# A fixed task order, w3 and w4 in groups of two token blocks, and block transposes by DMA through DRAM instead of TensorE

## The chip, the cores and the metric

The kernel runs on one core of one Trainium2 chip. The metric is device time in microseconds (us), the median of several executions. In this text PE is TensorE (PEld its weight loads), DVE is VectorE, ACT is ScalarE, POOL is GpSimd and SP is SyncE, whose queue issues the DMAs. "SPq" in the profile is SP's sequencer while it issues.

## The reference

```python
def _A_ref(q, k, v, shift_k, ssm_k, ssm_D):       # S = 2048 tokens, D = 512
    ...                                           # k_shift: causal taps of k, 4 wide
    kv = k_shift * v
    y = irfft(rfft(pad(kv)) * rfft(pad(ssm_k)))[:S]        # long convolution, per channel
    y = y + kv * ssm_D
    return q * y

def _B_ref(x, w1, w2, w3, w4):                    # F = 1792
    h = gelu(layernorm(x) @ w1)
    hs = concat(four quarters of h, moved by +1, -1, +2, -2 tokens) @ w2
    x1 = x + hs
    return x1 + gelu(layernorm(x1) @ w3) @ w4

x = A_q
h = x + _A_ref(layernorm(x), A_k, A_v, A_shift_k, A_ssm_k, A_ssm_D)
return h + _B_ref(layernorm(h), B_w1, B_w2, B_w3, B_w4)
```

## The kernel before

Tokens are held as 16 blocks of 128. The first half of the kernel (the "FFT stage") computes the convolution as matmuls with tables of sines. The second half has a mixer (inverse matmuls, gate, h, layernorm, w1, w2) and an MLP (layernorm, w3, w4). w1 and w3 contract over channels, so each of the 16 blocks of normed h ("hb") and of normed x1 ("lb") must be transposed first: 32 block transposes, each of four 128x128 pieces on PE into PSUM (`ptx`), then one copy to the buffer `rc` by ACT or DVE.

Each half is a list of tasks. A task names the engines that may run it with a cost in us, and a scheduler in the program picks the order while the kernel is built. The hardware then runs each engine's list in that order; an engine that waits for one task does not go around it.

```python
    plan = Plan({"mm": 6, "pt": 2, "lb": 6, "z": 4}, 300)     # second half; 300 rounds of list scheduling
    ...
    def transposes(key):
        def f(e):
            pt = tl[("pt",) + key] = ps_x.tile([P, DC, P], BF16, name="ptx", tag="ptx")
            for c in range(DC):
                nc.tensor.transpose(pt[:, c, :], tl[key][:, c * P:(c + 1) * P], ident[:])
        return f
    def tcopy(key, dstT, slot):
        def f(e):
            copy(e, dstT[:, :, slot * P:(slot + 1) * P], tl[("pt",) + key][:])
        return f
    def w3mm(g, fc):
        def f(e):
            pg = mm(("g", g, fc))
            for k in range(DC):                               # 512 tokens a matmul: four blocks
                nc.tensor.matmul(pg[:], lhsT=w3_sb[:, k, fc * P:(fc + 1) * P], rhs=lnT[:, k, g * 512:(g + 1) * 512],
                                 start=(k == 0), stop=(k == DC - 1))
        return f
    ...                                                       # cut
            for c in (b - 1, b):
                task(("hb", c), {"V": 0.33, "G": 1.0, "A": 0.71}, hbf(c), [("rr", p)])
                task(("LT", c), {"PE": 0.24}, transposes(("hb", c)), [("hb", c)], take="pt")
                task(("TE", c), {"A": 0.48, "V": 0.33}, tcopy(("hb", c), hnT, c), drop=("LT", c))
            for h in range(2):
                task(("W", p, h), {"PE": 0.92}, w1mm(p, h), [("TE", b - 1), ("TE", b)], take="mm")
    ...                                                       # cut; the same for lb with L, E and w3
```

## Time and profile before

| | before |
|---|---|
| median time | 244.74 us (4 runs, 244.01 to 246.14) |
| span of the profiled run | 241.9 us |
| PE busy | 225.2 us, 93% of the span |
| granted PE clock, mean | 0.979 |

First the profile page of the kernel before: busy time by engine, then the span in 40 slices with the busy tenths of PE and DVE and the granted PE clock.

```profile
PE 225.2 (93%) x1685; PEld 111.8 (46%) x1685; DVE 159.1 (66%) x328; ACT 138.1 (57%) x193; POOL 54.3 (22%) x98
...
PE   7999898869989985899999999999999999999994
...
DVE  6859998958999979999999952993522640012121
...
PEclk9999999979999999599999999999999999999999
```

The windows of the kernel before, one row per stage: start and end, then length, busy time and number of instructions of each engine, granted clock, DMA share, GB/s. The stages are the FFT stage, the turn to the mixer, the mixer up to the first w3, and the rest.

```profile
core 0: us, PE busy (x) PEld busy (x) DVE busy (x) ACT busy (x) POOL busy (x), PEclk, DMA share, GB/s
8.00:84.30 76.30, 69.02 (x722) 33.64 (x715) 66.29 (x96) 62.47 (x68) 14.88 (x18) 0.98 0.65 252
84.30:103.50 19.20, 15.15 (x130) 5.58 (x128) 16.97 (x43) 10.80 (x16) 9.39 (x15) 0.82 0.74 258
103.50:131.70 28.20, 28.11 (x265) 20.11 (x262) 27.01 (x71) 21.46 (x39) 17.34 (x31) 1.00 0.00 1
131.70:238.60 106.90, 106.65 (x537) 50.13 (x534) 43.40 (x91) 39.80 (x67) 10.16 (x17) 1.00 0.06 19
```

From 103.5 to 238.6 us PE is idle for only 0.3 us, while the DMA share is near zero (0.00 and 0.06). Work taken off PE there should shorten the kernel by its own length, and the DMA engines look like a free place to put it. The PE waits of the kernel before (who waited for whom: us in total, times, longest), of which these are the two longest:

```profile
PE pw L465 <- DMA rc<-ra: 2.5, 1, 2.5
PE mm L806 <- DVE rd L640: 2.5, 1, 2.5
```

And its block transposes by form (count, then busy us, mean ns of one, idle before; the lengths of matmuls in the trace overlap, so that four of 219 ns or more take only 0.22 us in the chain of waits):

```profile
L692 PE MATMUL ptx<-ident,rd 128*128 128x128 bf16 x64 | 6.1, 230 | 0.6 <-ACT rd L678 0.6
L692 PE MATMUL ptx<-ident,lb 128*128 128x128 bf16 x64 | 5.5, 219 | 0.1
```

Those four, 0.22 us of PE, are one block's worth.

### The profile page before, as it was taken

What the parts mean: (1) busy time and instruction counts of PE and PEld (TensorE: products, weight loads), DVE (VectorE), ACT (ScalarE), POOL (GpSimd) and SP (SyncE); (2) the same over time, 40 slices, a digit from 0 to 9 for tenths busy, and PEclk for the clock granted to TensorE, in tenths of its full rate; (3) what the DMA queues carried; (4) which work ended last, traced back from release to release, by engine and by line L of the source; (5) the groups of instructions that cost most, each with busy time, mean ns of one, the idle gap of its engine ahead of it and who ended that gap; (6) DMA issues with size and microseconds to landing.
All of it is one profiled execution on the core that took longest, in us unless ns stands there. A gap on an engine that the chain in (4) does not pass through costs nothing.

```text
span 241.9 us, 4308 instructions
## 1 busy us (share of the span) xinstructions
PE 225.2 (93%) x1685; PEld 111.8 (46%) x1685; DVE 159.1 (66%) x328; ACT 138.1 (57%) x193; POOL 54.3 (22%) x98
## 2 busy tenths in 40 slices
PE   7999898869989985899999999999999999999994
PEld 2576443433333432367676455445444444444441
DVE  6859998958999979999999952993522640012121
ACT  3953778869999974589657854254300266611000
POOL 3741303000100222996651420161000000000000
PEclk9999999979999999599999999999999999999999
DMA  6999827961363569600000000001011100000111
GB/s 165 396 420 427 335 83 310 388 267 43 133 217 130 168 213 391 191 0 3 0 3 0 1 0 3 0 1 43 3 43 43 43 3 0 0 22 24 43 43 43
DMA packets 11046, 28.07 MB, mean 116 GB/s; under 512 B 1809, under 2 KB 5650, under 8 KB 9490
## 3 DMA queue, kind: packets, MB, share of 16 engines
q1 hardware_dynamic: 10208, 26.74, 29.1%
q0 software_dynamic: 288, 1.05, 1.7%
q8 instruction: 13, 0.21, 0.3%
q10 hardware_dynamic: 530, 0.01, 0.1%
q14 instruction: 7, 0.06, 0.1%
HBM read 13.11 MB, written 2.10 MB: 63 GB/s over the span
## 4 chain that ended last, share of the span: by engine, by line
PE 65%; DVE 16%; DMA 10%; ACT 4%; issue 2%; POOL 2%; ACTq 0%; SPq 0%; DVEq 0%; POOLq 0%
PE mm L786 19%; PE mm L771 17%; DMA rb<-in_A_v_dram 5%; PE mm L706 5%; PE pv L554 5%; PE mm L731 4%; PE ptx L692 3%; PE pw L465 3%; DVE xk L441 3%; DMA ssk_bf<-in_A_shift_k_dram 3%; DVE st L635 3%; PE mm L618 3%; DVE q_sb L736 2%; DMA rc<-ra 2%; DVE qst L511 1%
## 5 line engine op out<-in xcount | busy, mean ns | idle before, releaser
L777 ACT ACTIVATE ra<-mm 128x512 bf16<-128x512 f32 x56 | 33.3, 596 | 47.9 <-PE mm L771 47.8
L771 PE MATMUL mm<-rc,rb 128*128 128x512 bf16 x224 | 51.1, 379 | 0.0
L786 PE MATMUL mm<-rt,ra 128*128 128x512 bf16 x224 | 49.3, 379 | 0.0
L794 DVE TENSOR_TENSOR ob<-mm,rd 128x512 bf16<-128x512 f32 x16 | 11.1, 692 | 54.1 <-PE mm L786 54.0
L786 PEld LDWEIGHTS <-ra 128*128 128x128 bf16 x224 | 21.9, 98 | 26.2
L771 PEld LDWEIGHTS <-rb 128*128 128x128 bf16 x224 | 21.5, 98 | 24.1
L326 ACT CAST rb<-pw 128x1024 bf16<-128x1024 f32 x16 | 16.3, 1064 | 2.6 <-PE pw L465 2.6
L554 PE MATMUL pv<-rb,rt 64*128 64x512 bf16 x128 | 16.5, 378 | 0.4 <-ACT rb L326 0.3
L706 PE MATMUL mm<-rc,rf 128*128 128x256 bf16 x128 | 16.1, 273 | 0.1
L731 PE MATMUL mm<-rf,rb 128*128 128x512 bf16 x64 | 15.8, 379 | 0.0
L736 DVE SCALAR_TENSOR_TENSOR q_sb<-rd,cr,mm 128x512 bf16<-128x512 bf16 x16 | 11.6, 727 | 5.6 <-PE mm L731 5.6
L432 PE MATMUL pk<-diag,rb 128*128 128x256 bf16 (+3 forms) x112 | 15.0, 288 | 0.2
L465 PEld LDWEIGHTS <-rf 128*64 128x64 bf16 x128 | 7.3, 116 | 14.9 <-issue 11.3
L326 ACT CAST ra<-pc 128x1024 bf16<-128x1024 f32 x13 | 12.5, 1023 | 2.3 <-PE pc L387 1.3
L706 PEld LDWEIGHTS <-rf 128*128 128x128 bf16 x128 | 12.2, 98 | 2.9 <-issue 0.6
L465 PE MATMUL pw<-rc,rf 128*64 128x512 bf16 x64 | 10.1, 407 | 3.6 <-DMA rc<-ra 2.5
L544 DVE TENSOR_TENSOR rb<-rb,rd 128x1024 bf16<-128x1024 bf16 x16 | 11.0, 685 | 3.6 <-ACT rb L326 3.6
L326 ACT COPY rc<-ptx 128x512 bf16<-128x512 bf16 x19 | 11.0, 592 | 3.9 <-PE ptx L692 3.9
L712 ACT ACTIVATE rb<-mm 128x512 bf16<-128x512 f32 x16 | 9.7, 618 | 6.0 <-PE mm L731 4.0
L629 ACT ACTIVATE z<-mm,qrs 128x512 f32<-128x512 f32 x16 | 10.3, 694 | 4.8 <-PE mm L618 4.4
L326 ACT CAST rc<-ph 128x1024 bf16<-128x1024 f32 x11 | 10.7, 1023 | 4.0 <-PE ph L387 3.9
L640 DVE SCALAR_TENSOR_TENSOR rd<-q_sb,qmv,z 128x512 bf16<-128x512 bf16 x16 | 11.8, 736 | 1.4 <-ACT z L629 1.4
(166 smaller groups left out, 342.3 us busy)
## 6 DMA issues: line engine op xcount, KB each, us to landing
rd<-rc SPq DMA_DIRECT2D x16, 256.0 KB, 4.5
rc<-ra SPq DMA_DIRECT2D x16, 256.0 KB, 3.3
ra<-rb SPq DMA_DIRECT2D x16, 256.0 KB, 2.5
ra<-in_A_ssm_k_dram SPq DMA_DIRECT2D x4, 512.0 KB, 6.8
ra<-in_A_k_dram SPq DMA_DIRECT2D x4, 512.0 KB, 8.8
rb<-in_A_v_dram SPq DMA_DIRECT2D x2, 1024.0 KB, 12.4
q_sb<-in_A_q_dram SPq DMA_DIRECT2D x2, 1024.0 KB, 10.6
out_dram<-ob SPq DMA_DIRECT2D x16, 128.0 KB, 1.8
```

Source lines behind the costliest of these rows:

```text
L326: nc.scalar.copy(o, i)
L432: nc.tensor.matmul(pk[:, i, P * (m + lo):P * (m + hi + 1)], lhsT=kT[:, c, b, 2:P + 2] if b >= 0 else kT[:, c, NB + b, 1:P + 1], rhs=diag[: ...
L465: nc.tensor.matmul(ps[64 * t:64 * t + 64, r, :], lhsT=ftab[:, kh, r, t, :], rhs=z[:, kh, t, :], start=True, stop=True)
L554: nc.tensor.matmul(ps[:, t, :], lhsT=tt[hs, min(x, 2), kh, :], rhs=pr[hs, x // 2, x % 2, :], start=(x == 0), stop=(x == 3))
L640: nc.vector.scalar_tensor_tensor(out=h_sb[:, b, :], in0=q_sb[:, b, :], scalar=qmv[:, b, 0:1], in1=tl["z", b][:], op0=SUB, op1=MUL)
L706: nc.tensor.matmul(pw_[:, j * 256:(j + 1) * 256], lhsT=w1_sb[:, k, m * P:(m + 1) * P], rhs=hnT[:, k, p * 256:(p + 1) * 256], start=(k == 0 ...
L731: nc.tensor.matmul(px[:], lhsT=shifted(m, b), rhs=w2_sb[:, m, :], start=(m == 0), stop=(m == DC - 1))
L736: nc.vector.scalar_tensor_tensor(out=x1[:, b, :], in0=hbm[:, b, :], scalar=tl["cr", b // 2][:, b % 2:b % 2 + 1], in1=tl["x", b][:], op0=MU ...
L771: nc.tensor.matmul(pg[:], lhsT=w3_sb[:, k, fc * P:(fc + 1) * P], rhs=lnT[:, k, g * 512:(g + 1) * 512], start=(k == 0), stop=(k == DC - 1))
L777: nc.scalar.activation(gbuf[:, g % 2, fc, :], tl["g", g, fc][:], ACT.Gelu_apprx_tanh)
L786: nc.tensor.matmul(po[:], lhsT=gbuf[:, g % 2, fc, i * P:(i + 1) * P], rhs=w4_sb[:, fc, :], start=(fc == 0), stop=(fc == FC - 1))
L794: nc.vector.tensor_tensor(out=ob[:], in0=tl["o", 4 * g + i][:], in1=xh1[:, b, :], op=ADD)
```

## The change

The intent is to take 20 of the 32 block transposes off the saturated PE: a block goes to a DRAM scratch by a plain store, and comes back by DMA with the transposition done on the way. The schedulers of both halves are replaced by one order over the whole kernel, made beforehand (by a search, it seems). Smaller w3 groups (two token blocks) let MLP work start earlier.

```diff
-    def solve(self):                      # and forward(), backward(): list scheduling
-        ...
     def emit(self):
-        best = self.solve()
-        for _, n in sorted(best[1]):
-            self.t[n]["fn"](best[3][n])
+        for x in ORDER.split():           # ORDER = "1D 3D 4D 12G 30P 7D ...": task number and engine
+            ...
+    HP, LP = 4, 2                         # first 4 mixer pairs and 2 MLP pairs stay on PE
+    scr = ctx.enter_context(tc.tile_pool(name="scr", bufs=1, space=DRAM)).tile([2 * NB, P, D], BF16, name="scr")
+    def stored(key, slot):
+        return lambda e: nc.sync.dma_start(scr[slot], tl[key])
+    def flipped(dstT, scr_lo, n, lo):
+        def f(e):
+            for c in range(DC):           # four transposing loads for a pair of blocks
+                nc.sync.dma_start_transpose(dstT[:, c, lo:lo + n * P],
+                                            scr[scr_lo:scr_lo + n, :, c * P:(c + 1) * P].rearrange("b p x -> (b p) x"))
+        return f
@@ mixer, and alike with L and E in the MLP @@
+                if p < HP:
+                    (LT on PE and TE by copy, as before)
+                else:
+                    task(("LT", c), {"D": 0.5}, stored(("hb", c), NB + c), [("hb", c)], lat=LAND)
+            if p >= HP:
+                task(("TE", b), {"D": 1.6}, flipped(hnT, NB + b - 1, 2, (b - 1) * P), [("LT", b - 1), ("LT", b)], lat=LAND)
@@ w3 @@
-    def w3mm(g, fc):                      # 4 groups of four blocks, 512 columns a matmul
+    def w3mm(g, f):                       # 8 groups of two blocks, 256 columns a matmul, two fc a PSUM bank
```

Cut: all the order but its start, costs retouched in other tasks, the q statistics and table load moved in the order, one dummy warm-up fewer, the first inverse matmuls split in two tasks.

## The prediction

> **What bounds the kernel before.** The windows by stage show TensorE as the limit nearly everywhere: from 103.5 to 238.6 us PE is busy 134.8 of 135.1 us, and the chain of waits gives it 65% of the span. From 8 to 84 us (FFT stage) it is busy 69 of 76 us; the waits list names gaps: 2.5 us for the exchange copies rc<-ra before the first pw, about 1 us each for xk, pc evictions and rd copies. The one large hole is 84.3 to 103.5 us: about 6 us of real inverse matmuls plus dummy warm-ups (L572, L806), waiting for the chain: last exchange landed about 88.5, gate z on ACT 89.2, h on DVE from 89.9, pow on POOL 95.1, hb on ACT 97.4, transpose 98.3. DVE is 95% busy from 90 to 140 us; each h block costs it 1.6 us in series.
>
> **What changes, costed.**
> 1. 20 of 32 blocks lose their PE transposes. Four take 0.22 us of PE in the chain of waits, so 20 x 0.225 = 4.5 us leave a saturated PE. Their PSUM copies (ACT 586 ns, DVE 425 ns) go too. The Trainium skill (VectorE: DVE Perf Modes, "The three transpose paths") gives 390 ns per 128x128 transpose on TensorE, 1309 ns by DMA; here PE pays only about 56 ns of issue each, so the exchange wins less than that table suggests.
> 2. Added: 20 stores to DRAM, 40 transposing loads. The trace has 1.8 us from issue to landing for a 128 KB store; the skill (DMA: Bandwidth & Descriptors, "Anatomy of one DMA") calls about 2 us fixed. I estimate 6 us from hb to transposed data, against about 1 us now. The DMA engines are idle there (share 0.00 at 103.5 to 131.7): bandwidth is free, latency is not.
> 3. w3 at 256 columns instead of 512: the 256-column w1 matmuls take 0.87 us per eight, the 512-column ones 0.864 per four. Cost about 0.5 us.
> 4. One order across both halves: more pg matmuls before the first pw, two fewer q statistics in the DVE-bound part, one dummy group fewer. I estimate 1 to 3 us out of the FFT gaps. Splitting the inverse gains almost nothing: its matmuls already waited singly.
>
> **Critical path.** The first h starts at the same place, less the FFT gain. The order finishes four h before the first statistics (before: three), 1.5 us later; W of the fifth pair waits for DMA, about 5 us later than before. So PE gets new holes of 2 to 4 us between 105 and 122 us, but w3 starts about 122 us instead of 131.7 and fills the rest. From there about 113 us of PE work remain, without reason to stall; the tail (w4, 0.7 us add, store) is unchanged. Sum: -4.5 (transposes) +0.5 (w3) -2 (FFT) +0.5 (holes against earlier w3) = -5.5 us.
>
> **Prediction: 239.5 us**, 8 times in 10 within 235 to 244.5. Faster by over 2%: 0.55; within 2%: 0.41; slower: 0.04.
>
> **What would show it.** PE transposes ptx fall from 128 to 48; pv ends 1 to 3 us earlier; PE windows show holes before the first w3 near 122 us, none after; store-to-transposed latency near 6 us; eight 256-column w3 matmuls at 0.87 us.
>
> **What would make it wrong.** Slower transposing DMAs: the order is fixed, so each late block stalls everything behind it on PE, and stores on the same queue wait too. Or the search found more of the FFT and 84 to 103 us gaps than I credit (then nearer 235). Or 256-column matmuls not hiding their weight loads (98 ns against 108).

## The result

The changed kernel takes 262.0 us (4 runs, 260.74 to 263.36), against 244.74 us before. Ratios here are the mean time of one kernel's fast runs over that of the other's in the same rounds, so they are not quite the ratio of the medians quoted: here 1.070, 95% interval 1.061 to 1.079. The change is 7% slower; a gain of 2% was predicted.

The profile page of the changed kernel, the same rows as before:

```profile
PE 228.2 (87%) x1807; PEld 129.9 (50%) x1825; DVE 154.4 (59%) x317; ACT 134.1 (51%) x186; POOL 50.4 (19%) x98
...
PE   7899999899999849876997876999999866999994
...
PEclk9999999999999999995699979899999999799999
```

Where PE stood at 9 without a break in the second half, there are now three dents, and the granted clock falls there too. The windows of the changed kernel: the FFT stage, the turn and first mixer blocks up to the first store, the mixer to the next stores, then two stretches to the end.

```profile
8.00:80.30 72.30, 69.15 (x723) 32.16 (x719) 65.17 (x94) 62.29 (x66) 14.08 (x18) 1.00 0.68 262
80.30:107.60 27.30, 21.13 (x223) 11.07 (x225) 26.12 (x72) 19.23 (x33) 15.38 (x27) 1.00 0.57 191
107.60:131.20 23.60, 18.59 (x109) 11.75 (x109) 15.64 (x36) 10.71 (x19) 7.66 (x16) 0.78 0.20 56
131.20:205.50 74.30, 67.29 (x434) 43.82 (x439) 33.32 (x74) 23.40 (x41) 10.97 (x20) 0.95 0.19 52
205.50:258.00 52.50, 46.57 (x290) 29.23 (x292) 8.44 (x14) 14.36 (x25) 0.00 (x0) 0.97 0.14 41
```

The FFT stage is better than before: pv ends at 80.3 us instead of 84.3, and the first h starts at 86.0 us instead of 89.9. All of the loss comes after the first store to DRAM at 107.6 us, in stretches where PE is idle and the DMA engines are four fifths idle as well. The PE waits of the changed kernel show who is waited for:

```profile
PE mm L665 <- DMA rc<-scr: 8.3, 10, 1.1
PE mm L732 <- DMA rc<-scr: 7.6, 8, 1.1
```

The transposes by form of the changed kernel show that 80 of the 128 did leave PE:

```profile
L641 PE MATMUL ptx<-ident,rd 128*128 128x128 bf16 x32 | 3.0, 220 | 3.8 <-ACT rd L627 2.9 <-POOL rd L629 0.9
L641 PE MATMUL ptx<-ident,lb 128*128 128x128 bf16 x16 | 1.8, 266 | 0.0
```

So the intended work is gone from PE; in its place no single wait for the scratch is longer than 1.1 us, but there are eighteen of them. The timeline of the changed kernel, PE and the DMA queue alone, around one pair (start, length, engine, line; in brackets the idle time before and what ended it), shows why:

```profile
start us, us, engine line op out<-in xcount [idle before <-releaser]
...
147.38 3.81 SPq L655 DMA_TRANSPOSE rc<-scr  x3
149.01 0.27 PE L665 MATMUL mm<-rc,rf 128*128 128x256 bf16 x1
149.80 0.27 PE L665 MATMUL mm<-rc,rf 128*128 128x256 bf16 x1 [0.52 <-DMA rc<-scr]
...
151.13 0.27 PE L665 MATMUL mm<-rc,rf 128*128 128x256 bf16 x1 [1.06 <-DMA rc<-scr]
151.29 0.52 SPq L756 DMA_DIRECT2D out_dram<-ob  x1
151.91 0.87 SPq L650 DMA_DIRECT2D scr<-lb  x2
152.34 1.01 PE L665 MATMUL mm<-rc,rf 128*128 128x256 bf16 x4 [0.93 <-DMA rc<-scr]
```

PE does one w1 matmul, waits, does the next: it marches at the beat of the queue, one of four column chunks every 1.2 to 1.3 us. The instructions on the scratch give the beat (duration of the issue in ns, min/median/max, first and last start), and the landing time from issue:

```profile
L655 SPq DMA_TRANSPOSE rc<-scr x40: 1104/1234/1961, 110.7 to 220.0; - x40
L650 SPq DMA_DIRECT2D scr<-lb x12: 332/400/523, 138.8 to 213.7; - x12
L650 SPq DMA_DIRECT2D scr<-rd x8: 332/396/879, 107.6 to 139.7; - x8
...
DMA to landing us min/median/max: 1.7/2.4/3.9
```

A transposing load holds the queue for 1.23 us, a plain store for 0.40. A pair of blocks so takes 4 x 1.23 = 4.9 us of queue where the task's cost says 1.6, and the 40 loads take 49 us in all, during which nothing else can be issued on that queue.

### The profile page after: what moved, and what is told of

The parts are those of the page before. It is cut to its first block, busy times and chain, and to the rows that moved or that the text cites. A ratio compares the mean times of both kernels' runs of the same rounds, so it can differ in the third digit from the quotient of the medians.

```text
span 261.4 us, 4638 instructions
## 1 busy us (share of the span) xinstructions
PE 228.2 (87%) x1807; PEld 129.9 (50%) x1825; DVE 154.4 (59%) x317; ACT 134.1 (51%) x186; POOL 50.4 (19%) x98
## 5 line engine op out<-in xcount | busy, mean ns | idle before, releaser
L732 PE MATMUL mm<-rc,rb 128*128 128x256 bf16 x448 | 56.0, 284 | 7.8 <-DMA rc<-scr 7.6
L738 ACT ACTIVATE ra<-mm 128x512 bf16<-128x512 f32 x56 | 32.5, 596 | 50.6 <-PE mm L732 50.6
L732 PEld LDWEIGHTS <-rb 128*128 128x128 bf16 x448 | 45.5, 102 | 18.4 <-issue 9.9
L665 PE MATMUL mm<-rc,rf 128*128 128x256 bf16 x128 | 20.1, 300 | 9.0 <-DMA rc<-scr 8.3
L665 PEld LDWEIGHTS <-rf 128*128 128x128 bf16 x128 | 13.3, 106 | 14.4 <-issue 11.7
L490 PE MATMUL pv<-rb,rt 64*128 64x512 bf16 x128 | 17.1, 377 | 1.4 <-ACT rb L265 0.9
L690 PE MATMUL mm<-rf,rb 128*128 128x512 bf16 x60 | 16.7, 405 | 1.2 <-ACT rb L671 0.7
L578 ACT ACTIVATE z<-mm,qrs 128x512 f32<-128x512 f32 x16 | 10.5, 689 | 5.6 <-PE mm L567 3.8
L609 POOL TENSOR_TENSOR rr<-uw,mhalf 128x4 f32<-128x4 f32 x8 | 9.6, 1197 | 18.1 <-DVE hm L598 18.1
L371 PEld LDWEIGHTS <-rb 128*128 128x128 bf16 x112 | 9.3, 98 | 7.5 <-issue 2.1
L265 ACT CAST rb<-pv 128x1024 bf16<-128x1024 f32 x12 | 12.8, 1099 | 0.0
L380 DVE TENSOR_TENSOR xk<-pk,rb 128x1024 bf16<-128x1024 f32 x8 | 9.8, 1223 | 3.4 <-DMA rb<-in_A_v_dram 1.6
## 6 DMA issues: line engine op xcount, KB each, us to landing
q_sb<-in_A_q_dram SPq DMA_DIRECT2D x2, 1024.0 KB, 10.5
```

The costliest lines, as they stand in the source:

```text
L265: nc.scalar.copy(o, i)
L371: nc.tensor.matmul(pk[:, i, P * (m + lo):P * (m + hi + 1)], lhsT=kT[:, c, b, 2:P + 2] if b >= 0 else kT[:, c, NB + b, 1:P + 1], rhs=diag[: ...
L490: nc.tensor.matmul(ps[:, t, :], lhsT=tt[hs, min(x, 2), kh, :], rhs=pr[hs, x // 2, x % 2, :], start=(x == 0), stop=(x == 3))
L578: nc.scalar.activation(z[:], tl["y", b][:], ACT.Identity, bias=1.0, scale=qrs[:, b:b + 1])
L665: nc.tensor.matmul(pw_[:, j * 256:(j + 1) * 256], lhsT=w1_sb[:, k, m * P:(m + 1) * P], rhs=hnT[:, k, p * 256:(p + 1) * 256], start=(k == 0 ...
L690: nc.tensor.matmul(px[:], lhsT=shifted(m, b), rhs=w2_sb[:, m, :], start=(m == 0), stop=(m == DC - 1))
```

## The experiments

The theory (A): the queue time of the transposing loads, which is a cost per instruction, makes every pair late, and the fixed order has nothing else for PE at those places. Rivals: (B) the fixed order or the 256-column w3 is itself bad; (C) the round trip through DRAM (store, landing, load, landing) is too slow, whatever the queue does.

| run | what | median us | ratio to before (95%) |
|---|---|---|---|
| after | the changed kernel | 262.0 | 1.070 (1.061 to 1.079) |
| r1_pe_same_order | all transposes on PE | 241.73 | 0.986 (0.981 to 0.991) |
| r2_plain_copy | plain loads, wrong data | 236.59 | 0.965 (0.962 to 0.968) |
| r3_merged | one transposing load a pair | 236.72 | 0.966 (0.959 to 0.974) |
| r4_split | eight a pair, single look | 307.53 | |
| r5_before_one_load | kernel before, one a pair | 242.43 | 0.989 (0.986 to 0.992) |
| r6_before_four_loads | kernel before, four a pair | 244.82 | 0.999 (0.995 to 1.004) |
| r7_from_sbuf | two a pair, no DRAM trip | 236.13 | 0.963 (0.960 to 0.967) |
| r11_more_dma | r7 with 24 blocks by DMA | 238.91 | 0.974 (0.969 to 0.979) |

**r1_pe_same_order.** The changed kernel with `HP, LP = 8, 8`; in the order, each store is replaced by its PE transposes and each load by copies (mixer on ACT, MLP on DVE).

> The changed kernel with all 32 block transposes back on TensorE; the fixed order and the two-block w3 groups stay. Theory A (the queue time of the transposing loads, 1.24 us each and 4.96 us a pair, makes PE wait): the FFT gain of about 3.9 us is kept, so 238 to 242 us. Rival B (the fixed order or the 256-column w3 is itself bad): 250 us or more.

Measured 241.73 us. Rival B falls: without the DMA path the order and the small groups are 1.4% faster than before. Its w3 matmuls start at 120.7 us, those of the kernel before at 131.5. (The order was not made anew for transposes on PE, so 241.73 us need not be the best that such a kernel can do.)

**r2_plain_copy.** Wrong data: the same stores, the same number of loads of the same bytes, but without transposition.

```diff
-                nc.sync.dma_start_transpose(dstT[:, c, lo:lo + n * P],
-                                            scr[scr_lo:scr_lo + n, :, c * P:(c + 1) * P].rearrange("b p x -> (b p) x"))
+                nc.sync.dma_start(dstT[:, c, lo:lo + n * P].rearrange("p (b x) -> p b x", b=n),
+                                  scr[scr_lo:scr_lo + n, :, c * P:(c + 1) * P].rearrange("b p x -> p b x"))
```

> Wrong result on purpose: each transposing load is a plain copy of the same bytes from the same DRAM scratch, same count, same waits. Theory A: the issue falls to 0.4 to 0.5 us each, a pair takes 2 us instead of 5, time 236 to 242 us. Rival C (the round trip through DRAM itself, store and landing of 2 us each, is too late for this order): 252 us or more. Rival B: near 262 us.

Measured 236.59 us, so 25 us come back when only the kind of load changes. Its line on the scratch (as above, with the landing time, which here and above is that of stores and loads together):

```profile
L655 SPq DMA_DIRECT2D rc<-scr x40: 360/465/548, 112.0 to 193.4; - x40
...
DMA to landing us min/median/max: 1.7/2.0/3.5
```

The loads hold the queue 0.47 us instead of 1.23, while the landing time is nearly the same: for the loads alone, the DMA lists of the two runs have medians of 2.2 us and 2.4. Rival C falls: the trip through DRAM stayed, and it costs this order nothing. The comparison with the reference passed this kernel although its data are wrong.

**r3_merged.** One transposing load for a pair, right data:

```diff
-            for c in range(DC):
-                nc.sync.dma_start_transpose(dstT[:, c, lo:lo + n * P],
-                                            scr[scr_lo:scr_lo + n, :, c * P:(c + 1) * P].rearrange("b p x -> (b p) x"))
+            nc.sync.dma_start_transpose(dstT[:, :, lo:lo + n * P], scr[scr_lo:scr_lo + n].rearrange("b p x -> (b p) x"))
```

> Right result: one transposing load per pair (256 rows by 512 columns) instead of four of 256 by 128. If the 1.24 us is a cost of the instruction: a pair takes 1.3 to 2 us of the queue, time 238 to 244 us, better than before. If it is a cost per transposed piece or byte: one issue lasts about 5 us, time stays 258 to 264 us.

**r4_split.** Eight a pair:

```diff
-                nc.sync.dma_start_transpose(dstT[:, c, lo:lo + n * P], ...)
+                for i in range(n):
+                    nc.sync.dma_start_transpose(dstT[:, c, lo + i * P:lo + (i + 1) * P], scr[scr_lo + i, :, c * P:(c + 1) * P])
```

> Right result: eight transposing loads per pair (128 rows by 128 columns each) instead of four. Cost per instruction: about 1.24 us each, 9.9 us a pair, time 285 us or more. Cost per piece or byte: about 0.65 us each, time 260 to 268 us.

Measured 236.72 us merged and 307.53 us split. The lines of the transposing loads, first of the merged kernel, then of the split one:

```profile
L654 SPq DMA_TRANSPOSE rc<-scr x10: 1227/1233/1330, 111.8 to 192.0; - x10
```

```profile
L656 SPq DMA_TRANSPOSE rc<-scr x80: 1093/1230/2531, 110.6 to 264.9; - x80
```

The issue lasts 1.23 us for 32 KB (128x128, split), 64 KB (256x128, changed kernel) and 256 KB (256x512, merged). The issue is thus a cost of the instruction, not of bytes or pieces. The landing does depend on the size: 2.4 us after issue for 64 KB and 3.3 for 256 KB. But a merged pair is there 3.3 us after its load begins, where the last of four loads, begun 3.7 us after the first, lands some 6.1 us after it. The same bytes moved with 10, 40 and 80 such instructions give 236.7, 262 and 307.5 us (the last a single look). The merged kernel did better than the 238 to 244 us expected of it. The windows of the merged kernel show that the dents are gone: PE is idle for less than 1 us between 108.4 and 131.2 us, and for 0.3 us in the 69 us after that.

```profile
8.00:80.30 72.30, 69.31 (x722) 32.22 (x719) 65.30 (x96) 62.33 (x66) 14.11 (x18) 1.00 0.67 263
80.30:108.40 28.10, 22.68 (x213) 11.78 (x215) 26.15 (x72) 18.48 (x32) 16.08 (x29) 0.88 0.54 184
108.40:131.20 22.80, 21.87 (x177) 16.30 (x178) 21.11 (x52) 16.48 (x29) 10.62 (x21) 1.00 0.30 77
131.20:200.00 68.80, 68.54 (x487) 47.92 (x490) 30.71 (x63) 26.71 (x46) 7.82 (x14) 1.00 0.26 68
```

**r5_before_one_load and r6_before_four_loads.** Here the DMA path alone is put into the kernel before, with its own scheduler and its four-block groups, for the same 20 blocks. The scheduler is told the measured queue cost: 1.3 us a pair for one load, 5.0 us for four.

```diff
+                else:
+                    task(("LT", c), {"D": 0.5}, stored(("hb", c), NB + c), [("hb", c)], lat=1.9)
+            if p >= HP:
+                task(("TE", b), {"D": 1.3}, flipped(...), [("LT", b - 1), ("LT", b)], lat=2.1)    # r6: 5.0 and lat=1.2
```

> The kernel before, its own scheduler and four-block w3 groups; only the same 20 blocks go through DRAM, with one transposing load per pair, and the scheduler is told the measured costs (1.3 us of queue a pair, 2.1 us to land). If the transposes themselves gain what they take from PE (4.5 us), 239 to 242 us. If the exchange is worth it only in the searched order, 244 us or more.

> As the run before, but with four transposing loads per pair as in the changed kernel, and the scheduler is told the true 5.0 us a pair. If an honest cost in the scheduler would have saved the change, 240 to 244 us. If 50 us of queue time in stretches with a deadline cannot be hidden, 246 to 256 us: slower than before, but less than the changed kernel's 262, whose order believed 1.6 us a pair.

Measured 242.43 and 244.82 us. Exchanging PE transposes for merged loads gains 1.1% by itself in this schedule, a little less than the 239 to 242 us expected. Four loads a pair gain nothing (0.999, interval 0.995 to 1.004), but they also lose nothing when the scheduler knows what they cost: 40 issues of 1.24 us are in that trace too, and its PE waits list has none for the scratch. The time fell between my two expectations, close to the 240 to 244 us for an honest cost, and below the 246 to 256 us for a cost that cannot be hidden. So the cost of the instruction alone does not explain the 17 us that the changed kernel lost against the kernel before: the order matters too. That it was the 1.6 us in place of 4.9 which made the order so sensitive is argued, not shown: r6 differs from the changed kernel also in its scheduler and its w3 groups, and neither was the fixed order made anew with the true cost, nor the scheduler told the wrong one.

**r7_from_sbuf.** From the merged kernel, the store and the scratch go; each block is transposed straight from on-chip memory, two loads a pair.

```diff
-        return lambda e: nc.sync.dma_start(scr[slot], tl[key])
+        return lambda e: None
-            nc.sync.dma_start_transpose(dstT[:, :, lo:lo + n * P], scr[scr_lo:scr_lo + n].rearrange("b p x -> (b p) x"))
+            for i, key in enumerate(keys):
+                nc.sync.dma_start_transpose(dstT[:, :, lo + i * P:lo + (i + 1) * P], tl[key])
```

> The merged kernel without the trip through DRAM: each block is transposed by one load straight from on-chip memory (two transposing loads a pair, no stores). Queue time a pair 2.5 us against 2.0 with the stores, latency about 2 us less. If the DRAM trip is off the critical path, as the merged kernel's lack of PE waits for DMA says, 235 to 238.5 us. If the trip still costs (rival C), 234 us or less. If a block with an on-chip source costs more than 1.24 us, slower than 239.

Measured 236.13 us, the same as the merged kernel within noise. The trip through DRAM is off the critical path, as r2 said, and is not needed. With this source the instruction costs the same:

```profile
L655 SPq DMA_TRANSPOSE rc<-lb x12: 1190/1216/1716, 129.4 to 188.8; - x12
L655 SPq DMA_TRANSPOSE rc<-rd x8: 1200/1257/1924, 108.0 to 133.3; - x8
```

**r8_verify, r9_verify_control, r10_verify_sbuf.** As r2 passed with wrong data, passing proves little about a transposition. These three have a test at the end. Each of the 20 blocks is read back from the scratch, transposed on PE and compared with what the DMA wrote; the squared differences, times 10000, are added to one block of the output. Times of no interest (292.76, 294.66 and 293.07 us; r8 took 56 us more than the merged kernel, not the 30 expected).

> The merged kernel with a test at its end: each of the 20 stored blocks is transposed on TensorE and the squared difference from what the DMA wrote, times 10000, is added to one output block. Correct if the merged load transposes exactly; far off otherwise. Time about 30 us over the merged kernel, of no interest.

> Control, wrong on purpose: the same test at the end of the kernel with plain copies. The comparison with the reference passed for the plain copies without the test, so it does not see untransposed blocks by itself; with the test it must now be far off, else the test of the merged kernel proves nothing.

> The same test at the end of the kernel that transposes straight from on-chip memory (its stores are kept for the test alone). Correct if those loads transpose exactly. Time of no interest.

r8 (merged) and r10 (from on-chip memory) came out correct, and the control on the plain copies was wrong by a relative error of 102877.9. So the merged load and the on-chip source do transpose, within what the comparison can see after the factor of 10000. The changed kernel itself, with four loads a pair, was not put to this test; it passed only the comparison that wrong data pass too.

**r11_more_dma.** r7 with `HP, LP = 2, 2`: the third and fourth mixer pairs go by DMA too, at the place of their PE transposes in the order.

> From on-chip memory as before, and the third and fourth pairs of the mixer go by DMA too (24 of 32 blocks). If only PE work counts, 0.9 us less, 235 us. If latency counts where PE has nothing else to do (it waits 3 us for the first hb there), their W come 2 us later and it is the same or slower, 235.5 to 239 us.

Measured 238.91 us, slower than r7. The PE waits of this run:

```profile
PE mm L665 <- DMA rc<-rd: 3.2, 1, 3.2
PE ptx L642 <- ACT rd L628: 3.0, 1, 3.0
```

The second line stands in r7 too (3.0 us); the first is new. PE has no other work there in this order, so the time from hb to landed data counts, and PE transposes are right; w3 starts at 122.7 us against 119.6 in r7. This is the second of the two outcomes expected. How much of the 3.2 us is queue and how much landing, the run does not separate.

## Why the prediction was wrong

**The step that failed** is point 2 of the prediction: "bandwidth is free, latency is not", with "about 6 us from hb to transposed data". Bandwidth and latency were both about right: stores landed in 1.8 to 1.9 us, loads 2.4 us after issue, the DMA engines stayed mostly idle. A third cost, the time of the issuing queue, was left out of the sum. It measured 1.23 us for each transposing load, 49 us for 40. For the first pair of the changed kernel, the first store is issued at 107.6 us and the loads begin at 110.7; the fourth load is issued some 3.7 us later and lands 2.4 us after that, and PE's wait for it ends at 116.9: 9.3 us, not 6. The second pair stands behind the first in the queue, and PE's wait for it ends 5.2 us later still. The prediction named slower transposing DMAs as what would make it wrong, but gave slower a chance of 4%. The number was even quoted: "1309 ns by DMA" from the Trainium skill (VectorE: DVE Perf Modes, "The three transpose paths"). It was set against PE's 56 ns and put aside. Taken as the price of one load and multiplied by the 40 loads of the diff, it would have been an estimate of 52 us of one serial queue, where the trace then showed 49. But the page gives it for a 128x128 piece, and each of these loads moves two; counted by pieces the estimate would have been 105 us. That the price is one of instructions, only r3 and r4 showed.

**"from there ... without reason to stall"** failed with it. The holes before 122 us were nearly foreseen (2 to 4 us; of the PE waits for `rc<-scr`, 4.1 us lie there). But the trace has more such waits at 137 to 139 us, 149 to 163 us and 205 to 223 us, 11.9 us in all.

**The rest of the loss.** The changed kernel is 26.0 us longer in span than the merged one (261.4 against 235.4). Both have 1807 matmuls on PE; the merged kernel's page, to set against that of the changed kernel above, says:

```profile
PE 220.2 (94%) x1807; PEld 127.9 (54%) x1825; DVE 154.0 (65%) x317; ACT 134.0 (57%) x186; POOL 51.2 (22%) x98
```

In the changed kernel PE is idle 18.0 us longer (33.2 against 15.2), of which 15.9 us are waits for the scratch (8.3 + 7.6), and busy 8.0 us longer with as many matmuls (228.2 against 220.2). The granted clock accounts for about that much, by an estimate: in the three windows after 107.6 us, (1 - clock) times length is 5.2 + 3.7 + 1.6 = 10.5 us, some of which coincides with the waits; the merged kernel has 3.4 us of the same kind, from 80.3 to 108.4 us. The Trainium skill (TensorE: Matmul & The Clock Gate, Part 1) says that the array's clock is set by how busy it has lately been and is halved when it has been idle. This stretch of the trace fits the first; the halving it shows with PE half busy, not idle: from 114 to 118 us PE is busy 2.14 of 4 us, and from 118 to 122 us 1.97 of 4 us at a granted clock of 0.50; it comes back to 1.00 after 130 us. That the clock fell because of the waits was not tested by a run of its own.

Point by point:

- *Transposes off PE, -4.5 us.* Right in the searched order: r1 to r3, 241.73 to 236.72, is -5.0 us, though r1's order was not made for its transposes. In the kernel before it was worth only 2.7 us (r5).
- *w3 at 256 columns, about +0.5 us.* In the saturated stretch from 181.47 to 183.21 us of the changed kernel, sixteen such matmuls take 1.74 us, so 0.87 per eight, as predicted: the weight loads are hidden.
- *FFT stage, -1 to -3 us.* Too small: the first h starts 3.9 us earlier (86.0 against 89.9).
- *w3 near 122 us instead of 131.7.* 120.7 us in r1 and 120.8 in r3; 127.5 in the changed kernel, where w1 groups that wait for DMA stand before it in PE's order.
- *The sum.* With the queue time mended (r3) the change is worth 3.4%, more than the 2.1% forecast; 5.5 us were summed, 8 came.

## What to carry to other kernels

Cost a DMA three ways: bytes over bandwidth, time to landing, and the time its issuing queue is held; the last was per instruction here, so count instructions in the diff and multiply. A fixed order is only as good as the costs it was made for: with the same order, loads of 4.9 us a pair gave a 7% loss and loads within the 1.6 us that its costs name (r3) a 3.4% gain. Under a scheduler that was told their price (r6), four loads a pair cost nothing against the kernel before. Before trusting a correct result, ask whether the comparison would notice the part you changed.

The best versions here are the merged load (236.72 us) and the load straight from on-chip memory (236.13 us), 3.4 and 3.7% faster than before; their loads passed the test of transposition.

## What the Trainium skill lacked or had wrong

- DMA: Bandwidth & Descriptors, "DMA Transpose (X-bar)": the section gives no issue cost (the page has one only in sequencer cycles of "previous generations", beside its trn3 figures). On this chip a transposing load held the SP queue 1.23 us, whether it moved 32, 64 or 256 KB from DRAM, and 1.22 to 1.26 us for 128 KB from on-chip memory; a plain load of 64 KB held it 0.47 us.
- Advanced Engine Details and Errata, "X-Bar Transpose (TRN2)", says that transposing DMAs are as fast as regular ones. For loads of 64 KB the landing nearly was (2.4 us against 2.2 at the median), the issue was not (1.23 us against 0.47), and 40 of them made 262.0 us against 236.59 us with plain loads.
- VectorE: DVE Perf Modes, "The three transpose paths": the 1309 ns for a 128x128 transpose by DMA is near the 1.23 us seen for the issue of one instruction, but the table doesn't say that a four to eight times larger transpose in one instruction holds the queue no longer. Its 390 ns on TensorE is not what a stream of them costs: four took 0.22 us of PE here.
- TensorE: Matmul & The Clock Gate, "Why this matters for your kernels" warns of idle gaps over about 3 us. That is not all that matters: here the clock fell to 0.50 at about 118 us after waits of at most 1.1 us, which left PE busy 2.14 of 4 us, while a single gap of 2.9 us before 95.4 us in the same trace left it at 1.00. (The same page tells elsewhere of frequent short idles that do this.)
